# A new order for the first 740 steps of a hand-ordered retention and SwiGLU kernel

## The chip, the cores and the metric

One core of one Trainium2 chip runs the kernel. The metric is the device time of one execution in microseconds (us); lower is better. The engines have short names below: PE (TensorE, matrix products), DVE (VectorE), ACT (ScalarE), POOL (GpSimd) and SP (SyncE, which here does nothing but issue transfers).

## What is computed

Two blocks, one behind the other. The first is a recurrent retention over 4 batches, 8 heads, 768 positions and 64 values per head; the second is a SwiGLU feed-forward block over the 3,072 tokens that come out of it, with 512 model values and 1,536 inner ones.

```python
for t in range(S):                       # q, k, v: (4, 8, 768, 64)
    state = gamma[None, :, None, None] * state + np.einsum('bhd,bhe->bhde', k[:, :, t], v[:, :, t])
    y[:, :, t] = scale * np.einsum('bhd,bhde->bhe', q[:, :, t], state)
...
x = np.ascontiguousarray(attn_out.transpose(0, 2, 1, 3)).reshape(B * S, H * D)
...
g = x @ w_gate                           # (3072, 512) @ (512, 1536)
silu = g * (1.0 / (1.0 + np.exp(-g)))
val = x @ w_val
return (silu * val @ w_out).astype(np.float32)
```

The weights come as 8-byte numbers, because a float32 array is multiplied by a NumPy double when they are made; a load of one 128 x 512 piece is 512 KB.

## The kernel before

**Tiling.** The sequence is cut into 24 chunks of 128 positions (4 batches of 6). The chunks are worked through in four segments (`NSEG`) of six chunks each; a segment has 2 x 384 tokens. Each segment goes through three stages: retention of its six chunks, the up stage (gate and value products for 12 blocks of 128 inner values, SiLU, product) and the down stage (12 blocks, summed in six PSUM banks, one for each 128 tokens). Each float32 product is made from three passes of a narrower format: operands are split by `near_a`, `near_b`, `near_c` (weights and inner values) or `far_a`, `far_b`, `far_c` (inputs), the first on ACT, the second on DVE and the third on POOL or DVE.

**The first segment is special.** In it the weights are also loaded in 8-byte form, turned into float32, summed for a seven-product scheme that the later segments use, and kept in DRAM (`wup`, `wdn`, `wdnt`). So its up stage takes plain products (`plain`, `plain_part`). While its down stage runs, the retention of the second segment runs beside it.

**What sets the order.** Nothing is ordered by a scheduler at run time. `PLAN` is a string of 2,368 step names; `run` walks through it and issues what each name stands for. Each engine runs its own instructions in just the order in which they are issued, and waits by semaphores for what they need. A step thus has a place in the queue of each engine that it uses, and all that stands behind it on that engine waits with it. All loads and stores go out on SP's queue in order of the plan, apart from two loads of `q` that ACT issues at the very start. In the trace the transfers use eight semaphores in turn, and the issue of each waits until the transfer eight places before it has landed.

The steps that the text below names, with the line of the instruction in the trace:

- `l c:w` loads a chunk (0 to 5) of the first segment: `w` is 0 for keys, 1 for queries, 2 for values, 3 for keys by rows (256 KB each, line 485). `A n` loads a part of the decay table. `U f`, `V f` load weights (line 532): `f` 0 to 11 for the up blocks, 12 to 17 for pairs of down blocks. `Z` stores made weights (lines 503, 580), `P n` and `1/l n` load chunks of the second segment (line 935), `L` a column of decays.
- Retention: `s c` scores (PE line 651, DVE line 657), `o c` the old state's part (728), `m c` the new part and the first input split (742, ACT line 1138), `t c` the state's update (713; DVE line 718), `r c` transposes of keys (692), `x c:1`, `x c:2` the other two input splits (DVE). `q`, `k`, `K`, `Q`, `E`, `g` scale by decays.
- Weights: `a`, `b`, `c` (ACT lines 553, 556, 559), `S`, `C` (DVE lines 566 and 574, or POOL line 576) turn 8-byte words into float32; `n f:0` to `n f:5` split them; `T f:0` to `T f:2` sum them (DVE).
- Up stage: `p f:j`, `v f:j` are gate and value products for a third of the tokens (blocks 0 and 1, PE line 1075); `G f:i`, `W f:i` the same for half of the tokens (blocks 2 to 11, line 1057). `i f:i` is the SiLU (ACT), `j f:i` the product (DVE). `G f:i` uses bank `i`, `W f:i` bank `2 + i`; `G f:i` therefore waits until `i` of the block before has read its bank.
- Down stage of the first segment: `0/W f` loads down weights, `0/d f.0` to `0/d f.2` split them (ACT, POOL or DVE, DVE), `0/h f.0` to `.2` split the inner values, `0/D f.tok` multiplies (PE line 1301), `0/Z f` stores.
- Retention of the second segment: `1/sc`, `1/A`, `1/B`, `1/C` on PE (line 825), `1/dec`, `1/q`, `1/k`, `1/was`, `1/new`, `1/y`, `1/sum` and `1/x` on the other engines. `1/p f.n` are the seven products of its up stage (line 1230).

Of the kernel before, what the change touches and what calls it, by code (L numbers as in the profile page):

```python
# [25 lines left out]
L = 3  # L26
# [31 lines left out]
    C1:1 g3 b1:0 n1:0 v0:0 l5:0 U2:3 s5 S1:0 t3 c1:0 C1:0 l5:2  # L58
    p0:1 n1:1 u0:0 u0:1 T0:0 q5 v0:1 a2 l4:2 b2 y0:1 o5 y0:0
    o4 n1:3 S2 n1:2 m5 T0:1 n1:4 c2 m4 n1:5 x5:2 p1:0 l5:3  # L60
    x5:1 p1:1 u1:0 C2 v1:0 U3:1 T0:2 x4:2 T1:0 U12:0 a3 v1:1 y1:0
    x4:1 T1:1 L b3 p0:2 a12 c12 n2:0 S3 u1:1 T1:2 b12 u0:2
    U4:3 c3 Z0 n2:1 v0:2 Z1 n2:3 S12 y1:1 a4 n2:2 p1:2 v1:2
    C3 u1:2 n2:4 G2:0 y0:2 C12 G2:1 n3:0 U13:1 y1:2 n3:1 n2:5 b4
    T2:0 n3:2 S4 U5:2 n3:3 c13 T2:1 W2:0 Z12 W2:1 h0 c4 i2:1
    n3:4 i2:0 G3:0 n3:5 T3:0 C4 T2:2 T3:1 U6:3 j2:0 a5 G3:1 T3:2
    j2:1 Z2 n4:0 U7:0 W3:0 i3:0 n4:1 b5 n4:2 n4:3 S5 n4:4 W3:1
    i3:1 n4:5 c5 G4:0 C5 n5:0 a6 b6 a13 l4:3 T4:0 j3:0 G4:1
    n5:1 j3:1 Z3 T4:1 n5:3 i4:0 n5:2 T4:2 S6 W4:0 b13 c6 i4:1
    n5:4 a7 S13 C6 W4:1 n6:0 T5:0 U8:2 Z4 b7 U14:3 n5:5 n6:1  # L70
    G5:0 j4:1 S7 C13 j4:0 G5:1 n6:2 a8 n6:3 P2 n6:4 i5:1 c14
    W5:1 i5:0 Z13 c7 j5:1 T6:0 n6:5 W5:0 a14 U9:1 U15:0 C7 T5:1
    G6:0 T6:1 n7:0 T5:2 G6:1 n7:3 n7:1 T6:2 i6:0 b8 j5:0 Z5 S8
    n7:4 W6:1 b14 g4 n7:2 G7:0 i6:1 W6:0 P0 c8 S14 C8 Z6
    C14 h2 a9 b9 G7:1 j6:1 n7:5 S9 n8:0 c15 n8:3 j6:0 k5
    c9 W7:1 Z14 T7:0 n8:1 C9 n8:4 U10:2 a15 n8:2 i7:1 U11:1 W7:0
    T7:1 j7:1 n8:5 i7:0 T8:0 T7:2 b15 Z7 S15 a10 n9:0 G8:0 G8:1
    W8:1 i8:0 n9:3 b10 j7:0 T8:1 n9:1 n9:2 U16:3 S10 a11 n9:4 G9:0
    k4 i8:1 t4 C15 c10 C10 n9:5 W8:0 g5 n10:0 T8:2 T9:0 b11
    c16 n10:1 G9:1 Z15 j8:0 j8:1 n10:2 a16 n10:3 t5 U17:2 b16 W9:0  # L80
    i9:1 T9:1 0/h0.0 T9:2 S11 Z8 W9:1 S16 G10:1 n10:4 i9:0 C16 c11
    C11 n10:5 n11:0 j9:0 Z9 G10:0 n11:3 Z16 i10:1 j9:1 a17 i10:0 W10:1
    P1 n11:4 T11:0 T11:1 1/was0.0 T11:2 n11:1 W10:0 Z11 c17 n11:2 n11:5 b17
    0/h0.1 0/W0 G11:1 0/h1.0 G11:0 j10:0 0/d0.0 h1 0/h0.2 1/sc0 j10:1 i11:0 0/h1.1
    0/W1 S17 0/d1.0 i11:1 0/d0.1 1/l3 C17 T10:0 1/dec0.0 W11:0 0/d1.1 0/d0.2 W11:1
# [240 lines left out]
T0, UP0 = 30.0, 8.35  # L326
# [1176 lines left out]
```

## Time and profile before

| what | value |
|---|---|
| median of 3 runs | 639.5 us (638.78 to 642.62) |
| span of the profiled execution | 641.7 us |
| mean granted TensorE clock in it | 0.997 |
| first matmul of the first up stage (line 1075) | 22.87 us |
| first matmul of the first down stage (line 1301) | 132.25 us |
| first matmul of the second segment's up stage (line 1230) | 195.79 us |

The profile gives no time for the profiled execution besides its span; the span lies 2.2 us above the median of the runs and within their spread. Numbers with a place on the time axis are in us from the start of that span. A row of a timeline reads: start, duration, engine and line, operation, what it writes and reads, how many instructions the row joins, and in square brackets the idle time of the engine before it and what ended that. A row of a list of waits reads: who waited for whom, then total time, number of times and the longest.

### The profile page before, as it was taken

What the parts mean: (1) busy time and instruction counts of PE and PEld (TensorE: products, weight loads), DVE (VectorE), ACT (ScalarE), POOL (GpSimd) and SP (SyncE); (2) the same over time, 40 slices, a digit from 0 to 9 for tenths busy, and PEclk for the clock granted to TensorE, in tenths of its full rate; (3) what the DMA queues carried; (4) which work ended last, traced back from release to release, by engine and by line L of the source; (5) the groups of instructions that cost most, each with busy time, mean ns of one, the idle gap of its engine ahead of it and who ended that gap; (6) DMA issues with size and microseconds to landing.
All of it is one profiled execution on the core that took longest, in us unless ns stands there. A gap on an engine that the chain in (4) does not pass through costs nothing.

```text
span 641.7 us, 14131 instructions
## 1 busy us (share of the span) xinstructions
PE 630.8 (98%) x5601; PEld 581.7 (91%) x5601; DVE 506.9 (79%) x764; ACT 396.6 (62%) x845; POOL 173.2 (27%) x117
## 2 busy tenths in 40 slices
PE   7999999999999999999899999999999999999997
PEld 6899999987789999997788999998888999999886
DVE  4998788899898889887489777978778888877551
ACT  4786897677866665667376664756764655564220
POOL 0544455544423531210001343340002014232000
PEclk9999999999999999999899999999999999999999
DMA  9899998689788443688783435577785345304764
GB/s 319 289 353 311 372 333 274 259 323 305 281 278 305 140 157 115 214 263 239 204 312 130 179 115 206 173 203 229 229 290 196 113 149 189 128 13 140 230 212 149
DMA packets 57747, 143.03 MB, mean 223 GB/s; under 512 B 5840, under 2 KB 28368, under 8 KB 57680
## 3 DMA queue, kind: packets, MB, share of 16 engines
q1 hardware_dynamic: 57104, 141.33, 64.5%
q8 instruction: 44, 0.72, 0.5%
q10 hardware_dynamic: 576, 0.79, 0.3%
q14 instruction: 23, 0.19, 0.1%
HBM read 112.21 MB, written 29.88 MB: 221 GB/s over the span
## 4 chain that ended last, share of the span: by engine, by line
PE 94%; DMA 5%; ACT 1%; SPq 1%; issue 0%; DVE 0%; ACTq 0%
PE bank L1230 41%; PE bank L1301 30%; PE bank L1057 13%; PE bank L825 5%; PE bank L1075 3%; DMA oitem<-wdnt 2%; DMA hT<-in_v_n_dram 2%; PE bank L742 1%; DMA hT<-in_q_t_dram 1%; PE bank L728 0%; SPq L820 0%; PE bank L713 0%; PE bank L651 0%; ACT gitem L1129 0%; ACT local L871 0%
## 5 line engine op out<-in xcount | busy, mean ns | idle before, releaser
L1301 PE MATMUL bank<-oitem,gitem 128*128 128x512 f32 (+1 forms) x873 | 205.9, 393 | 3.0 <-DMA oitem<-wdnt 2.9
L1301 PEld LDWEIGHTS bank<-oitem,gitem 128*128 128x128 f32 x873 | 161.9, 189 | 38.1 <-DMA oitem<-wdnt 3.5
L1230 PE MATMUL bank<-xa,gitem 128*128 128x384 f32 x864 | 160.6, 334 | 0.0
L1230 PEld LDWEIGHTS bank<-xa,gitem 128*128 128x128 f32 x864 | 150.6, 188 | 0.1
L1135 POOL TENSOR_TENSOR gitem<-gitem 128x768 fp32r<-128x768 f32 x36 | 72.1, 2007 | 185.0 <-DVE gitem L1132 165.7
L1135 POOL TENSOR_TENSOR oitem<-oitem 128x512 fp32r<-128x512 f32 (+1 forms) x48 | 52.8, 1105 | 168.1 <-DVE oitem L1132 148.0
L418 DVE SCALAR_TENSOR_TENSOR gitem<-gitem 128x768 fp32r<-128x768 f32 x84 | 86.6, 1041 | 1.7 <-DVE gitem L1132 0.5
L1057 PE MATMUL bank<-xa,oitem 128*128 128x384 f32 x480 | 84.2, 335 | 0.0
L1230 PE MATMUL bank<-xb,gitem 128*128 128x384 f32 x432 | 83.7, 335 | 0.0
L1057 PEld LDWEIGHTS bank<-xa,oitem 128*128 128x128 f32 x480 | 83.0, 188 | 0.2
L1230 PEld LDWEIGHTS bank<-xb,gitem 128*128 128x128 f32 x432 | 75.8, 188 | 0.4
L1129 ACT ACTIVATE gitem<-loads 128x768 fp32r<-128x768 f32 x72 | 59.1, 842 | 25.7 <-PE bank L1230 16.9
L1132 DVE SCALAR_TENSOR_TENSOR gitem<-gitem,loads 128x768 fp32r<-128x768 f32 x72 | 70.5, 991 | 3.4 <-ACT gitem L1129 3.3
L1132 DVE SCALAR_TENSOR_TENSOR gitem<-gitem,hT 128x768 fp32r<-128x768 f32 x48 | 46.2, 965 | 28.0 <-ACT gitem L1129 24.1
L1129 ACT ACTIVATE gitem<-hT 128x768 fp32r<-128x768 f32 x48 | 40.2, 844 | 43.7 <-PE bank L1301 35.3
L1230 PE MATMUL bank<-xb,oitem 128*128 128x384 f32 x216 | 43.0, 335 | 0.0
L1230 PEld LDWEIGHTS bank<-xb,oitem 128*128 128x128 f32 x216 | 38.0, 188 | 0.0
L1246 ACT COPY tmp<-bank 128x384 f32<-128x384 f32 x36 | 17.3, 480 | 27.0 <-PE bank L1230 22.9
L1247 DVE TENSOR_TENSOR hT<-bank,tmp 128x384 f32<-128x384 f32 x36 | 20.0, 554 | 16.5 <-PE bank L1230 16.4
L1245 ACT COPY tmp<-bank 128x384 f32<-128x384 f32 x36 | 17.2, 479 | 24.8 <-PE bank L1230 17.1
L1249 DVE TENSOR_TENSOR hT<-hT,bank 128x384 f32<-128x384 f32 x36 | 19.7, 550 | 13.4 <-ACT bank L1249 13.2
L1247 ACT COPY tmp<-bank 128x384 f32<-128x384 f32 x36 | 17.3, 481 | 16.5 <-PE bank L1230 11.9
(152 smaller groups left out, 807.2 us busy)
## 6 DMA issues: line engine op xcount, KB each, us to landing
loads<-wup SPq DMA_DIRECT2D x36, 896.0 KB, 5.4
oitem<-wdnt SPq DMA_DIRECT2D x33, 768.0 KB, 4.7
wdnt<-oitem SPq DMA_DIRECT2D x12, 768.0 KB, 5.8
wup<-first SPq DMA_DIRECT2D x9, 896.0 KB, 6.9
rawp<-in_w_gate_dram SPq DMA_DIRECT2D x12, 512.0 KB, 7.3
rawp<-in_w_val_dram SPq DMA_DIRECT2D x12, 512.0 KB, 6.6
rawp<-in_w_out_dram SPq DMA_DIRECT2D x12, 512.0 KB, 5.8
out_dram<-chunk_x SPq DMA_DIRECT2D x21, 256.0 KB, 4.7
```

The costliest lines, as they stand in the source:

```text
L418: stt(o, x, 1.0, y, op0=mul, op1=op)
L825: nc.tensor.matmul(o, a, b, start=start, stop=True, skip_group_check=True)
L1057: nc.tensor.matmul(o, w[:, a, ts(b, P)], X0[:, a, i, NC - 1 - b], start=a == b == 0, stop=a == 2 and b == NC - 1, skip_group_check=True)
L1075: nc.tensor.matmul(o, w[:, a, ts(b, P)], X0[:, a, :, NC - 1 - b, ts(j, P)], start=a == b == 0, stop=a == 2 and b == NC - 1, skip_group_che ...
L1129: act(o[0], x, AF.Copy, scale=CUT / FAR)
L1132: stt(o[1], f32(o[0]), -FAR, x, op0=mul, op1=add)
L1135: op(o[2], f32(o[0]), f32(o[1]), op=add)
L1230: nc.tensor.matmul(o, w[:, a, k], x[:, a, KH - 1 - k], start=start and a == k == 0, stop=a == 2 and k == KH - 1, skip_group_check=True)
L1246: lambda: act(gate, c11, AF.Silu, scale=ONE), lambda: copy(u2, x),
L1247: lambda: copy(p5, wb), lambda: tt(h1, x, p5, op=add),
L1249: lambda: act(x, x, AF.Silu, scale=ONE), lambda: tt(h1, h1, x, op=mul))
L1301: nc.tensor.matmul(o, hs[g][:, a, ds(i * TH + u * P, P)], wo[g][:, a, cols], start=n == 0 and (f == 0 or final), stop=f == NF - 1 and a == ...
```

## The change

The first 740 names of `PLAN` are put in another order: 696 of the first 740 places hold another name than before, and from the 741st on the string is the same. The names are the same, each once. No function, size, buffer or number changes elsewhere. What a step does depends on the plan only where buffers are taken in turn: the two halves of banks 0 to 3 for `p` and `v`, the score buffers, and the slots of `item`, which go round in the order in which they are asked for.

The old string has 13 names a line and the new one is filled to a width, so that a diff shows every line as changed. Its beginning, old and new:

```diff
-    A0 I0 l0:0 l1:0 A2 A1 U0:0 s0 a0:1 r1 l0:2 s1 b0:1
-    A4 A3 l2:1 l2:0 r0 m0 K0 S0:1 c0:1 l1:2 x0:1 t0 s2
-    E1 l3:0 l3:1 m1 l2:3 C0:1 g2 V0:0 a0:0 Q2 n0:0 b0:0 l2:2
-    x1:2 s3 x1:1 n0:1 l4:1 l4:0 l3:2 t1 S0:0 k2 x0:2 q3 c0:0
-    C0:0 o2 U1:1 m2 o3 n0:3 s4 m3 a1:1 n0:4 x2:1 l5:1 l3:3
-    b1:1 x2:2 x3:1 S1:1 t2 n0:2 p0:0 q4 a1:0 x3:2 c1:1 n0:5 k3
...
+    A1 A2 l0:0 A0 l0:2 l1:0 s0 U0:0 a0:1 I0 l2:0 s1 A4 b0:1 r0 K0 m0 S0:1 l3:1 l2:1 A3 l1:2 x0:2 r1
+    E1 x0:1 s2 t0 c0:1 g2 m1 l3:0 t1 V0:0 Q2 l2:3 C0:1 s3 x1:1 l3:2 q3 l3:3 k2 l2:2 a0:0 b0:0 S0:0
+    x1:2 n0:0 l4:1 o2 c0:0 n0:1 o3 l4:0 m3 C0:0 U1:1 n0:3 t2 m2 x3:1 n0:4 k3 g3 x2:1 l5:1 x2:2 s4
+    a1:1 n0:2 b1:1 S1:1 c1:1 l5:2 x3:2 C1:1 a1:0 n0:5 b1:0 l5:0 U2:3 t3 n1:0 p0:0 S1:0 v0:0 l4:2 q4
```

The queue of each engine is what is left when the names of its own steps are picked out. For PE, up to the last retention group of the first segment:

```
old: s0 r1 s1 r0 m0 t0 s2 m1 s3 t1 o2 m2 o3 s4 m3 t2 p0:0 v0:0 s5 t3 p0:1 v0:1 o5 o4 m5 m4 p1:0
new: s0 s1 r0 m0 r1 s2 t0 m1 t1 s3 o2 o3 m3 t2 m2 s4 t3 p0:0 v0:0 p0:1 v0:1 s5 o5 o4 m4 m5 p1:0
```

For SP, up to the loads of the fourth chunk:

```
old: A0 l0:0 l1:0 A2 A1 U0:0 l0:2 A4 A3 l2:1 l2:0 l1:2 l3:0 l3:1 l2:3 V0:0 l2:2 l4:1 l4:0 l3:2 U1:1 l5:1 l3:3
new: A1 A2 l0:0 A0 l0:2 l1:0 U0:0 l2:0 A4 l3:1 l2:1 A3 l1:2 l3:0 V0:0 l2:3 l3:2 l3:3 l2:2 l4:1 l4:0 U1:1
```

Where the up stage goes over into the down stage, PE and DVE:

```
old PE:  ... W10:1 W10:0 G11:1 G11:0 1/sc0 W11:0 W11:1 0/D0.2 0/D0.1 0/D0.4 0/D0.0 1/A0
new PE:  ... W10:1 W10:0 1/sc0 G11:1 G11:0 W11:1 W11:0 0/D0.0 0/D0.1 1/A0
old DVE: ... n11:1 0/h0.1 j10:0 0/h0.2 j10:1 0/h1.1 S17 T10:0 1/dec0.0 0/d0.2 j11:0 j11:1 1/dec0.1
new DVE: ... n11:1 j10:1 0/h0.1 T10:1 0/h0.2 1/q0.0 j10:0 1/dec0.0 0/h1.1 S17 0/d0.2 j11:1 j11:0 1/dec0.1
```

Among the moves over a longer way: on ACT `c7` comes ahead of `i5:0`, and `g5` and `h1` are issued earlier; on POOL `k4` is issued earlier; on SP `l4:3` and `P0` are issued earlier and `L`, `P2` and `Z9` later; on PE the last retention group of the second segment, `1/C2`, comes ahead of six of the `0/D` groups that stood before it.

More of the change, by code (lines that the diff above doesn't have):

```diff
@@ L69 @@
[L69 to L85, printed above, removed]
@@ new lines @@
+    n3:2 T2:1 i2:0 n3:3 n3:4 i2:1 U5:2 T2:2 C4 n3:5 j2:0 j2:1 a5 C12 n4:0 b5 G3:0 G3:1 S5 T3:0 n4:3
+    P0 W3:1 W3:0 U6:3 Z2 Z12 n4:4 i3:1 c5 n4:1 i3:0 j3:1 n4:2 G4:1 C5 j3:0 U7:0 a6 T3:1 b6 T4:0 T3:2
+    n5:0 T4:1 S6 c13 a13 n5:1 i4:1 G4:0 n4:5 Z3 c6 n5:3 i4:0 n5:2 n5:4 h0 W4:1 W4:0 n5:5 T4:2 j4:1
+    C6 T5:0 b13 W5:1 S13 G5:1 j4:0 a7 G5:0 b7 h1 S7 i5:1 n6:0 n6:1 j5:1 C13 U8:2 c7 C7 n6:3 Z4 T5:1
+    W5:0 a8 n6:4 n6:2 U14:3 G6:1 c14 Z13 i5:0 T5:2 n7:0 G6:0 U9:1 b8 a14 j5:0 L S8 i6:1 n6:5 W6:1
@@ L198 @@
[L198 to L201 removed]
+    3/mv0.0 3/B0 3/dec2.1 3/dec2.0 2/W2 2/D2.1 3/l7 3/was0.11 3/was0.10 3/y0.10 3/y0.11 3/begin
```

313 lines of the change are left out of this document (159 added, 154 removed).

## The prediction

> **What bounds the kernel now.** I read the page's head and its chain by engine first, then TensorE's list of waits over the whole span, the windows of the stretch that the new order covers, and last the timelines of single engines there.
>
> ```profile
> span 641.7 us, 14131 instructions
> ...
> PE 630.8 (98%) x5601; PEld 581.7 (91%) x5601; DVE 506.9 (79%) x764; ACT 396.6 (62%) x845; POOL 173.2 (27%) x117
> ...
> PE 94%; DMA 5%; ACT 1%; SPq 1%; issue 0%; DVE 0%; ACTq 0%
> ```
> ```profile
> PE bank L1301 <- DMA oitem<-wdnt: 2.9, 1, 2.9
> PE bank L651 <- DMA hT<-in_k_t_dram: 1.7, 2, 1.1
> PE bank L742 <- DMA hT<-in_v_n_dram: 1.4, 2, 0.9
> PE bank L1420 <- DVE warm L1435: 1.1, 1, 1.1
> PE bank L651 <- DVE tmp L657: 0.4, 1, 0.4
> ```
> ```profile
> 0.00:10.00 10.00, 7.23 (x66) 6.31 (x68) 2.91 (x6) 2.15 (x3) 0.20 (x4) 1.00 0.82 282
> 10.00:20.00 10.00, 8.27 (x142) 7.11 (x144) 8.94 (x15) 7.37 (x22) 3.42 (x3) 1.00 1.07 373
> 20.00:30.00 10.00, 10.00 (x131) 9.31 (x127) 9.20 (x17) 7.68 (x17) 5.37 (x5) 1.00 0.85 292
> 40.00:50.00 10.00, 10.00 (x76) 10.00 (x75) 9.81 (x15) 8.21 (x14) 5.88 (x4) 1.00 0.92 340
> 70.00:80.00 10.00, 10.00 (x60) 10.00 (x59) 6.82 (x10) 7.12 (x10) 4.12 (x3) 1.00 1.00 357
> 140.00:150.00 10.00, 10.00 (x147) 7.95 (x146) 9.30 (x15) 8.03 (x26) 4.05 (x3) 1.00 0.90 317
> 170.00:180.00 10.00, 10.00 (x132) 8.05 (x124) 10.00 (x15) 6.70 (x16) 5.79 (x4) 1.00 0.82 280
> ```
>
> TensorE (PE) carries 94% of the chain. The columns of the windows are PE, weight loads, VectorE (DVE), ScalarE (ACT), GpSimd (POOL), clock, DMA share and GB/s. From 20 us on PE is busy in each of them, and the list of waits has only one PE wait behind the start, the 2.9 us on `wdnt`, in a part whose order stays. So the 740 steps cover a stretch in which PE has idle time in its first 20 us alone: 1.7 + 1.4 + 0.4 us there wait on transfers or on work that follows them (the 1.1 us before the warm-up comes ahead of the first step). The same window shows why: DMA at 1.07 of its engines' time, 373 GB/s. The start is paced by the order of the loads.
>
> **The change part by part.** No step is added or dropped, and no instruction changes its kind. The cost is in who waits for whom.
>
> *The start.* Here is PE's timeline, with the line of each group of matmuls:
>
> ```profile
> 5.93 1.16 PE L651 MATMUL bank<-hT 64*128 64x128 f32 x16 [1.14 <-DMA hT<-in_k_t_dram]
> 18.24 1.09 PE L742 MATMUL bank<-tmp,hT 128*64 128x128 f32 x16 [0.86 <-DMA hT<-in_v_n_dram]
> 19.27 1.09 PE L728 MATMUL bank<-loads,states 64*64 64x128 f32 x16
> 20.29 1.16 PE L651 MATMUL bank<-hT 64*128 64x128 f32 x16
> 21.38 1.09 PE L742 MATMUL bank<-tmp,hT 128*64 128x128 f32 x16
> 22.30 0.64 PE L713 MATMUL bank<-hT 128*64 128x64 f32 x16
> 34.49 11.78 PE L1075 MATMUL bank<-xa,oitem 128*128 128x256 f32 x96
> 46.11 58.41 PE L1057 MATMUL bank<-xa,oitem 128*128 128x384 f32 x336
> 132.25 3.13 PE L1301 MATMUL bank<-oitem,gitem 128*128 128x512 f32 x12
> ```
>
> The last wait of PE at the start ends at 18.24, when the values of chunk 2 (`l2:2`) land and `m2` can run. In the new order the same transfers stand ahead of `l2:2`, and two more, `l3:2` and `l3:3`, of 256 KB each. At the 373 GB/s of that window 524,288 bytes take 1.41 us, so `l2:2` lands at 18.24 + 1.41 = 19.65. For that, PE gets two groups done earlier that stood behind `m2`: `o3` (20.29 - 19.27 = 1.02 us) and `m3` (22.30 - 21.38 = 0.92 us), whose values now land ahead of `l2:2`. From 18.24 to `p1:0` at 34.49 PE has no wait, 16.25 us of work. So `p1:0` now starts at 19.65 + 16.25 - 1.02 - 0.92 = 33.96, 0.53 us earlier.
>
> A second, smaller term: a group of matmuls followed by one of the same array shape is shorter. `m3`, before `t2` of the same 128*64, takes 0.92 from start to start; `m2`, before `o3` of 64*64, takes 19.27 - 18.24 = 1.03. In the stretch left after `l2:2` the new order (`t2 m2 s4 t3 p0 ... s5 o5 o4 m4 m5 p1`) has seven changes of shape, where the old one without `o3` and `m3` has nine: two times 0.11 is 0.22 us. Together 0.75 us gained.
>
> Waits ahead of `l2:2` do not count in this sum, old or new (`s1` now has 512 KB more ahead of its keys, and will wait longer): they end before 19.65. Bounds of this part: it can gain no more than the transfer waits of the list without the one before `s0`, whose keys have the same 1,024 KB up to them as before: 1.7 + 1.4 + 0.4 - 1.14 = 2.4 us. And it loses 1.41 - 0.75 = 0.7 us if `l2:2` slips by as much again, two more 256 KB loads.
>
> *The stretch of the first matmul stage (46 to 132 us).* GpSimd and SyncE keep nearly their sequence. Weight loads `U7` and `U14` get 764 and 508 KB more ahead of them, at 357 GB/s 2.2 and 1.5 us. The nearest cover in the trace is this:
>
> ```profile
> 77.21 1.15 ACT L559 ACTIVATE rawp<-rawp 128x1024 int32<-128x1024 uint32 x1 [1.29 <-DMA rawp<-in_w_out_dram]
> 78.26 0.47 ACT L463 ACTIVATE tmp<-bank 128x384 f32<-128x384 f32 x1
> ```
>
> `c14` at 77.21 waits for `U14`, and `i5:0` (78.26 to 78.73) stands behind it and must free the bank of `G6:0`. `G6:0` is the 17th of 28 equal groups of the row at 46.11, so it starts at 46.11 + 16 x 58.41/28 = 79.49. With 1.5 us more, `i5:0` ends at 80.2; but `G6:0` comes behind `G6:1` now, one group (2.09 us) later, at 79.49 + 2.09 - 0.75 = 80.8. Hidden by 0.6 us; without that cover it would cost up to 1.5. Loads that move far (`l4:3` up, `P2`, `L` down) have cover on both sides: `P2`, the latest, now goes out right behind `P1`,
>
> ```profile
> 117.48 0.94 SPq L935 DMA_DIRECT2D loads<-in_q_t_dram x2
> ```
>
> which itself moves up; `P2` is first read by `1/A0`, behind 132 us. Counted at nothing.
>
> *Entry into the down stage.* This is the tightest place for VectorE:
>
> ```profile
> 118.28 0.69 DVE L1132 SCALAR_TENSOR_TENSOR oitem<-oitem,loads 128x512 fp32r<-128x512 f32 x1 [1.51 <-ACT oitem L1129]
> 122.90 0.56 DVE L463 TENSOR_TENSOR hT<-bank,tmp 128x384 f32<-128x384 f32 x1 [0.80 <-PE bank L1057]
> 128.98 2.31 DVE L1145 SCALAR_TENSOR_TENSOR oitem<-oitem 128x512 fp32r<-128x512 f32 x1
> 133.59 0.68 DVE L418 SCALAR_TENSOR_TENSOR loads<-loads,tab 128x512 f32<-128x512 f32 x1
> 138.33 1.50 DVE L418 SCALAR_TENSOR_TENSOR first<-first 128x256 f32<-128x256 f32 x1
> ```
>
> `0/d0.2` (128.98 to 131.29) makes the last part of the first down weights, 0.96 us before PE uses it at 132.25. Two steps are moved ahead of it: `1/q0.0` (0.68) and `T10:1` (1.50, the row at 138.33). If VectorE filled its queue without a gap, it would be late by 2.18 + 0.75 - 0.96 = 1.97 us. But VectorE stood idle for 1.51 + 0.80 = 2.31 us in this queue, and the two steps need neither of the things that it waited for. 2.31 covers 2.18, and what is left (0.96 - 0.75 = 0.21 us plus 0.13) is still positive. I take 0, with 2.0 us as the far end.
>
> *From there to 196 us.* The down groups and the second segment's retention come in another order, with the same work. VectorE is at 9.3 to 10.0 of 10 here, so it can just keep up with PE; the last retention group `1/C2`, behind which the next segment's inputs are summed, moves ahead of six down groups (row 132.25: 3.13/4 = 0.78 us each, so 4.7 us), which gives that end more room. 0, with up to 0.75 lost again where VectorE alone sets the end.
>
> Sum: 641.7 - 0.75 = 640.95 for an execution like the profiled one. That one is 2.2 us above the median of the runs, 639.5 (638.78 to 642.62); taken off the median it is **638.8 us**.
>
> **The rivals.**
>
> *VectorE late at the down stage (slower).* If the two idle stretches at 118 and 122 us don't fill, `0/d0.2` ends 2.0 us late and PE waits; with VectorE at 9.3 to 10.0 behind it, nothing makes that up: 639.5 - 0.75 + 2.0 = 640.8. It turns to a loss from 0.75 us of wait on. A longer wait has a further price here, which this trace has once:
>
> ```profile
> 305.00:310.00 5.00, 3.08 (x10) 2.47 (x11) 5.00 (x10) 2.80 (x8) 0.00 (x0) 0.82 1.05 261
> 310.00:315.00 5.00, 5.00 (x20) 4.07 (x19) 1.08 (x1) 0.00 (x0) 0.00 (x0) 0.84 0.30 89
> ```
>
> Behind the one wait of 2.9 us the granted clock was 0.82 and 0.84, a loss of 5 x 0.18 + 5 x 0.16 = 1.7 us. So a new wait of 3 us costs 4.7 and gives 639.5 - 0.75 + 4.7 = 643.5. The Trainium skill, page "TensorE: Matmul & The Clock Gate", section "Part 1: The HAM clock gate", says that PE falls to half clock after an idle window of about 3.4 us; by that rule a 3 us wait would mostly go free, and the time would stay at 641.8. The trace shows the drop behind 2.9 us. For this rival: the margins of 0.2 to 0.6 us above. Against: no wait of PE on VectorE but the 0.4 us of the list.
>
> *Nothing moves.* PE is full from 20 us, and VectorE at 10.00 in 170 to 180 could set the end whatever PE gains ahead: 639.5.
>
> *The start gains all (faster).* If both `s` and `m` waits fall away, 2.4 us: 637.1. If besides the 2.9 us on `wdnt` and its 1.7 us of clock fall out differently, 632.5. That part keeps its order, so I give it little.
>
> **How the numbers follow.** Forecast (637.8 to 640.2, its own 0.75 with the loss of 0.7 at the low end): 0.45. VectorE late or another new wait of the same kind (640.3 to 643.5): 0.28, and beyond, with several such waits and slow clock, above 645.9: 0.07. Nothing moves: 0.10, inside the forecast's range. Start gains all (636 to 637.8): 0.08; more than that, 0.02. The range 636.2 to 643.5 leaves out the two tails and the edge of the third case. One per cent is 6.4 us, about what a measurement of this kernel can tell from no change: faster than 633.1 needs the late wait and its clock as well, 0.02; slower than 645.9, 0.07; the rest, 0.91, within.
>
> **What would show it.** Right, if PE's wait for `in_v_n` ends near 19.7 us and is followed by an L713 group, L1075 x96 starts near 33.7 to 34.0 us, and L1301's first row has no wait, near 131.5. Wrong, if PE's list of waits gains a row on DVE, ACT or POOL between 25 and 196 us, or if the first L1230 row, at 195.8 before, is not earlier. A changed clock row near 308 us would move the time without saying anything on the order.

## The result, and the profile after

| | before | after |
|---|---|---|
| median, first set (15 runs each) | 639.31 us | 641.16 us |
| ratio, first set | | 1.0029 (95% interval 1.0016 to 1.0043) |
| ratio, a second set (12 runs against 26) | | 1.0041 (1.0022 to 1.0060) |
| profiled execution | span 641.7 us | 640.04 us, span 638.3 us |
| first `p1:0` product (line 1075; 1067 after) | 34.49 us | 34.91 us |
| first down product (1301; 1293) | 132.25 us | 132.85 us |
| first product of the second up stage (1230; 1222) | 195.79 us | 197.05 us |

The change costs about 2 us, 0.3%. That lies within 1% and in the range, but the forecast was a gain of 0.7 us, and a small loss came. The spans of the two profiles point the other way because the profile of before holds the 2.9 us wait on `wdnt` and its slow clock, which the profile of after doesn't have; up to the first product of the second up stage, where the orders meet again, the new one is 1.26 us behind.

In the new source each line number is 8 lower. TensorE's list of waits for the new kernel (who waited for whom: total us, times, longest) answers to that of before:

```profile
PE bank L643 <- DMA hT<-in_k_t_dram: 1.7, 2, 1.2
PE bank L1412 <- DVE warm L1427: 1.1, 1, 1.1
PE bank L1293 <- issue: 0.4, 1, 0.4
PE bank L817 <- issue: 0.2, 1, 0.2
```

The wait for the values, whose end the prediction moved to 19.65 us, isn't there at all. By this list alone the start has become better: 1.7 us of transfer waits in place of 1.7 + 1.4. PE's timeline shows what the list can't (start, duration, engine and line, operation, how many instructions, and the idle time before):

```profile
5.98 2.08 PE L643 MATMUL bank<-hT 64*128 64x128 f32 x16 [1.17 <-DMA hT<-in_k_t_dram]
8.62 2.08 PE L643 MATMUL bank<-hT 64*128 64x128 f32 x16 [0.55 <-DMA hT<-in_k_t_dram]
10.63 1.11 PE L684 MATMUL bank<-loads,hT 128*128 128x128 f32 x4
11.67 1.70 PE L734 MATMUL bank<-tmp,hT 128*64 128x128 f32 x16
13.30 0.66 PE L684 MATMUL bank<-loads,hT 128*128 128x128 f32 x4
13.89 1.16 PE L643 MATMUL bank<-hT 64*128 64x128 f32 x16
...
34.91 11.77 PE L1067 MATMUL bank<-xa,oitem 128*128 128x256 f32 x96
...
132.85 1.67 PE L1293 MATMUL bank<-oitem,gitem 128*128 128x512 f32 x6
141.24 3.79 PE L1293 MATMUL bank<-oitem,gitem 128*128 128x512 f32 x16 [0.39 <-issue]
197.05 2.27 PE L1222 MATMUL bank<-xb,gitem 128*128 128x384 f32 x12
```

Two things stand out. The groups of `s0` and `s1`, 16 equal matmuls each, take 2.08 us; the same group takes 1.16 at 13.89, and took 1.16 at 5.93 before. So PE ran at half clock until about 13 us, and from `s1` on was busy all that time, which is why no wait shows it. And `s1` starts at 8.62 (7.61 before), since its keys now come behind 512 KB more; from there to `p1:0` PE has no wait at all. The transfers no longer pace the start, PE does. The second thing is the stretch from the first down product to the second up stage: 197.05 - 132.85 = 64.20 us, where before had 195.79 - 132.25 = 63.54, with a wait of 0.39 at 141.24.

**The theory that follows.** (a) At the start: the late `s1` leaves PE idle between `s0` and `s1`, so the clock is half just where PE now has no slack, and that eats the gain. (b) In the down stage, the new order makes PE wait for split weights. The rival for (a): the order of loads and groups itself is worse, at any clock. The rival for (b): VectorE is full there, and any order in which PE comes earlier makes it wait. In the profile above the clock is half from `s0` on, ahead of the hole, so here the hole can only have kept it there; a fall behind the hole is seen in `start_new` and `new_again` below.

### The profile page after: what moved, and what is told of

It reads as the page before. It is cut to its first block, busy times and chain, and to the rows that moved or that the text cites. A ratio compares the mean times of both kernels' runs of the same rounds, so it can differ in the third digit from the quotient of the medians.

```text
span 638.3 us, 14136 instructions
## 1 busy us (share of the span) xinstructions
PE 631.5 (99%) x5601; PEld 583.2 (91%) x5601; DVE 506.9 (79%) x764; ACT 396.0 (62%) x845; POOL 174.6 (27%) x117
## 4 chain that ended last, share of the span: by engine, by line
PE 96%; DMA 2%; DVE 1%; SPq 0%; issue 0%; ACT 0%
PE bank L1222 41%; PE bank L1293 31%; PE bank L1049 12%; PE bank L817 6%; PE bank L1067 3%; PE bank L643 1%; PE bank L734 1%; DMA hT<-in_k_t_dram 1%; DMA oitem<-wdn 1%; PE bank L720 1%; PE bank L705 1%; PE bank L684 0%; DVE oitem L1137 0%; SPq L601 0%; DVE first L558 0%
## 5 line engine op out<-in xcount | busy, mean ns | idle before, releaser
L1124 DVE SCALAR_TENSOR_TENSOR gitem<-gitem,hT 128x768 fp32r<-128x768 f32 x48 | 49.4, 1034 | 22.2 <-ACT gitem L1121 18.3
L1238 ACT COPY tmp<-bank 128x384 f32<-128x384 f32 x36 | 17.3, 480 | 27.0 <-PE bank L1222 20.8
L1237 ACT COPY tmp<-bank 128x384 f32<-128x384 f32 x36 | 17.3, 480 | 24.1 <-PE bank L1222 16.4
L1133 POOL TENSOR_TENSOR oitem<-oitem 128x512 fp32r<-128x512 f32 x12 | 20.5, 1709 | 31.3 <-ACT oitem L1130 22.0
```

What stands on the lines that cost most here:

```text
L1124: stt(o[1], f32(o[0]), -FAR, x, op0=mul, op1=add)
L1133: op(o[1], f32(o[0]), x, op=sub)
```

## The experiments

Each kernel was timed in five rounds against the kernel before on the same chip, and profiled once. "Stretch" is the time from the first down product to the second up stage. The diffs show names of the plan, cut out of it without regard to its line breaks.

### Which part loses: each half alone

`start_new` takes the new order up to `p1:0` and then the remaining names as the old one has them; `start_old` the other way round.

```diff
-    A0 I0 l0:0 l1:0 A2 A1 U0:0 s0 a0:1 r1 l0:2 s1 b0:1
+    A1 A2 l0:0 A0 l0:2 l1:0 s0 U0:0 a0:1 I0 l2:0 s1 A4 b0:1 r0
...
+    y0:0 o5 o4 n1:3 n1:2 b2 S2 m4 m5 p1:0 T0:1 n1:4 c2 n1:5 x5:2 l5:3 x5:1 p1:1
```

> The new order up to p1:0, then the old order of all that is left. Theory A (the start is at fault: the hole between s0 and s1 leaves PE at half clock for s0, s1, r0 and m0): p1:0 starts about 0.4 us later than before (34.9 against 34.49 us), the first matmul of the second segment's up stage about 0.4 us later (196.2 against 195.79), time 0.4 to 1 us above the kernel before, and s0 and s1 take about 2.1 us each instead of 1.16. Theory B (the entry into the down stage is at fault): p1:0 no later than 34.5, time as before within 0.5 us. Theory C (nothing in the first 196 us, only the late wait on wdnt falls out more often): time as before or above it, with the first matmul of the second segment's up stage at 195.8.

> The old order up to p1:0, then the new order of all that is left. Theory A: p1:0 at 34.5, no waits of PE beyond those of before, time as before within 0.5 us. Theory B: p1:0 at 34.5, but 0/D0 and 0/D1 wait 0.4 us each as in the changed kernel, the second segment's up stage starts about 0.9 us later (196.7), time 0.9 us above the kernel before. Theory C: 195.8 and time as before.

Measured: `start_new` 641.12 us, ratio 1.0022 (1.0008 to 1.0037). `start_old` 640.43 us, 1.0010 (0.9996 to 1.0025). So the start with the old rest loses, clear of zero; for the rest alone a loss is likely in size but not clear. Not all of the first is the start: `start_new` comes to the second up stage at 197.88 us, 2.09 behind before, of which 0.86 is there at `p1:0` and 0.77 is a PE wait at 46.66, where its two orders are joined. `start_old` has `p1:0` at 34.12 and one wait of 0.41 us, at 160.18, not the two at the entry that theory B names (the new kernel's list has only one wait of 0.4 there). In `start_new` the windows view shows the clock (columns: stretch, length, then busy time of PE, weight loads, VectorE, ScalarE, GpSimd, the granted clock, DMA share, GB/s):

```profile
6.00:8.00 2.00, 1.11 (x16) 0.92 (x16) 0.85 (x2) 0.00 (x0) 0.00 (x0) 0.85 1.03 387
8.00:10.00 2.00, 1.45 (x14) 1.48 (x16) 0.57 (x2) 0.07 (x1) 0.00 (x0) 0.50 1.09 378
10.00:12.00 2.00, 2.00 (x14) 1.45 (x14) 1.37 (x3) 0.59 (x1) 0.00 (x0) 0.50 1.06 387
12.00:14.00 2.00, 2.00 (x19) 1.67 (x16) 1.21 (x2) 0.98 (x2) 1.17 (x1) 0.50 1.06 370
14.00:16.00 2.00, 2.00 (x35) 1.68 (x36) 1.66 (x3) 1.69 (x9) 0.10 (x1) 0.94 1.11 382
```

Here PE had full clock at `s0`, waited 1.44 us for `s1`, and ran at 0.50 from 7.4 to 14.2 us: 14 and 19 matmuls in 2 us in which PE is always busy, against 35 of another mix once the clock is back. The equal groups tell it more strictly: `s0` takes 1.16 us and `s1` 2.08. `p1:0` comes at 35.35 us.

### The clock alone: filling the hole

`new_warm` is the new kernel with five steps of warm-up matmuls (they multiply zeros, and nothing reads them) between `s0` and `s1`, and nine in place of seven ahead of the first step. `old_warm` has only the nine. `warm_start` is `start_new` with both.

```diff
-    A1 A2 l0:0 A0 l0:2 l1:0 s0 U0:0 a0:1 I0 l2:0 s1 A4 b0:1
+    A1 A2 l0:0 A0 l0:2 l1:0 s0 w w w w w U0:0 a0:1 I0 l2:0 s1 A4 b0:1
...
-    warm_up(7)
+    warm_up(9)
```

> The changed kernel with two more warm-up products ahead of s0 and five between s0 and s1, so that PE has no hole there (the products write a bank that nothing reads before it is written anew). Theory A: s0 and s1 take 1.16 us each, p1:0 starts at 33.7 to 34.0 us as forecast, and the time falls by about 1 us against the changed kernel, to 640.2. Theory B and C: s0 and s1 may be faster, but p1:0 or what comes behind it moves by less than 0.3 us and the time stays at 641.

> The kernel before with the two more warm-up products ahead of s0. A control for the one above: all theories expect no change, 639.3 within 0.5 us, with s0 at 5.9 to 6.0 us and 1.16 us long; if it is faster by 0.5 us or more, the old start too runs into the half clock in some executions.

> The new order up to p1:0 with the warm-up products that close the hole between s0 and s1, then the old order. Theory 1 (two faults: the half clock at the start, and the new order of the down stage, which keeps PE waiting): p1:0 at 33.4, first down matmul at 131.1, no PE wait in the down stage, 63.6 us in it, second segment's up stage at 194.7, time 1 us under the kernel before, 638.4. Theory 2 (VectorE or the transfers set the end of the down stage whatever the order): second segment's up stage stays at 195.8 to 196.5, time as before, 639.4, and PE waits in the down stage in the old order too.

Measured: `new_warm` 639.76 us, ratio 1.0007 (0.9992 to 1.0022); `old_warm` 639.22 us, 0.9993 (0.9981 to 1.0004); `warm_start` 639.30 us, 0.9994 (0.9974 to 1.0014). No load, buffer or data product differs between the new kernel and `new_warm`. PE's timeline of `new_warm`:

```profile
5.90 1.16 PE L644 MATMUL bank<-hT 64*128 64x128 f32 x16 [0.81 <-DMA hT<-in_k_t_dram]
6.99 1.38 PE L1413 MATMUL bank<-warm 128*128 128x128 f32 x10
8.37 1.16 PE L644 MATMUL bank<-hT 64*128 64x128 f32 x16
...
19.34 0.69 PE L706 MATMUL bank<-hT 128*64 128x64 f32 x16 [0.25 <-DMA hT<-in_v_n_dram]
...
33.35 11.77 PE L1068 MATMUL bank<-xa,oitem 128*128 128x256 f32 x96
```

`s1` is no earlier by more than 0.25 us (8.37 against 8.62), but it takes 1.16, and `p1:0` starts at 33.35, 1.56 us before that of the new kernel and 1.14 before the old one's. The rival for (a) falls, as far as `p1:0` is concerned. The old order with more warm-up has no gain to speak of (its `s0` took 1.47 us, its `p1:0` came at 34.62), so it isn't the longer warm-up as such.

### The same without extra work: the keys earlier

`new_k1` is the new kernel with one name moved; `start_k1` the same for `start_new`.

```diff
-    A1 A2 l0:0 A0 l0:2 l1:0 s0 U0:0 a0:1 I0 l2:0 s1
+    A1 A2 l0:0 l1:0 A0 l0:2 s0 U0:0 a0:1 I0 l2:0 s1
```

> The new order with one name moved: the load of the keys of chunk 1 (l1:0) goes out right behind that of chunk 0 (l0:0), as in the old order, ahead of A0 and l0:2. Theory (PE's clock falls because of the 1.4 us wait between s0 and s1): the keys of chunk 1 land about 1.4 us earlier, s1 runs at about 7.1 us without a long wait, s0 and the groups up to 14 us take their full-clock lengths (16 matmuls of scores in 0.9 to 1.2 us, none of 1.7), p1:0 starts at 33.3 to 34.0 us in place of 34.9, and the time is 1.0 to 1.5 us under that of the new order, 639.6 to 640.2, ratio 1.000 to 1.001. Rival (the start's loss is in the order of the values' loads or of PE's groups, not in the clock): s1 earlier, but p1:0 again at 34.8 to 35.3 us and the time at 641.1, ratio 1.003.

> The new order up to p1:0 with the keys of chunk 1 loaded right behind those of chunk 0, and the old order from there on. Theory (clock alone spoiled the start; the old order of the down stage adds no waits): like the start with filler products, but without them: full clock from 4 to 7 us on, p1:0 at 33.3 to 34.0 us, no PE wait between 130 and 196 us, first product of the second segment's up stage at 194.9 to 195.6 us, time 638.4 to 639.3, ratio 0.998 to 1.000. Rival (order of loads as such): p1:0 at 34.8 to 35.3, time 641.1, ratio 1.002.

Measured: `new_k1` 639.95 us, ratio 1.0003 (0.9982 to 1.0025), as the theory expected; `start_k1` 640.38 us, 1.0008 (0.9993 to 1.0022), over its range of 0.998 to 1.000. PE's timeline of `new_k1`:

```profile
6.05 2.06 PE L643 MATMUL bank<-hT 64*128 64x128 f32 x32 [1.23 <-DMA hT<-in_k_t_dram]
8.90 0.66 PE L684 MATMUL bank<-loads,hT 128*128 128x128 f32 x4 [0.80 <-DVE loads L677]
...
11.84 1.16 PE L643 MATMUL bank<-hT 64*128 64x128 f32 x16 [0.67 <-DMA hT<-in_q_t_dram]
...
33.32 11.77 PE L1067 MATMUL bank<-xa,oitem 128*128 128x256 f32 x96
131.08 1.55 PE L1293 MATMUL bank<-oitem,gitem 128*128 128x512 f32 x6
139.63 3.83 PE L1293 MATMUL bank<-oitem,gitem 128*128 128x512 f32 x16 [0.96 <-DVE first L410]
160.44 0.51 PE L1293 MATMUL bank<-oitem,gitem 128*128 128x512 f32 x1 [0.33 <-DVE oitem L1137]
...
196.41 2.27 PE L1222 MATMUL bank<-xb,gitem 128*128 128x384 f32 x12
```

The 32 matmuls of `s0` and `s1` run as one group, and `p1:0` starts at 33.32. `start_k1` gets 33.67, but then waits 1.06 us in two places at 42.9 and 45.3 us, where its two orders are joined, and is no clean test behind them. (`start_new` has 0.77 us at that joint, `warm_start` 0.17.)

### The hole in the old order

```diff
-    A0 I0 l0:0 l1:0 A2 A1 U0:0 s0 a0:1 r1 l0:2 s1 b0:1
+    A0 I0 l0:0 A2 A1 l0:2 l1:0 U0:0 s0 a0:1 s1 r1 b0:1
```

> The old order with the hole put in: the keys of chunk 1 are loaded behind A2, A1 and the values of chunk 0 (1,792 KB up to them, as in the new order), and s1 stands right behind s0, ahead of r1. Theory (clock): PE waits 1.3 to 1.5 us before s1, the clock falls to half from 7 to 8 us until 13 to 14 us, s1 and the next groups take 1.6 us or more in place of 0.9 to 1.2, p1:0 starts 0.5 to 1.7 us later than 34.5, and the time is 0.5 to 1.7 us over that of the old order, ratio 1.001 to 1.003. Rival (the transfers pace the start, and PE's clock ahead of the values of chunk 2 is hidden by their landing): s1 may be late and slow, but p1:0 stays at 34.3 to 34.6 and the ratio is 1.000.

Measured: 640.51 us, ratio 1.0009 (0.9992 to 1.0025), not clear of zero. In its profile `s0` and `s1` take 2.08 us each, the clock is full only from 10.2 us on, and `p1:0` starts at 35.00, 0.51 later than before. But the wait ahead of `s1` is 0.35 us, not the 1.3 to 1.5 that was expected, and the clock is half already at `s0`, ahead of it: this profile doesn't show a hole bringing the clock down, and the time leaves the theory open too.

### The unchanged new order again

> The new order unchanged, beside the three others on one chip. Theory (the wait ahead of s1 costs the clock): ratio 1.002 to 1.004 again; in the profile groups of scores of 1.6 us or more somewhere between 6 and 14 us, p1:0 at 34.7 to 35.4, and the stretch of the down stage at 64.2 us or more with PE waits of 0.3 us or more. Rival (the first profile caught the clock by chance): all groups at full-clock length, p1:0 at 33.3 to 34.0, and a ratio near 1.000.

Measured: 642.19 us against 640.20, ratio 1.0041 (1.0022 to 1.0060). PE's timeline:

```profile
6.03 1.16 PE L643 MATMUL bank<-hT 64*128 64x128 f32 x16 [1.21 <-DMA hT<-in_k_t_dram]
8.63 2.08 PE L643 MATMUL bank<-hT 64*128 64x128 f32 x16 [1.44 <-DMA hT<-in_k_t_dram]
...
34.24 11.77 PE L1067 MATMUL bank<-xa,oitem 128*128 128x256 f32 x96
131.99 1.55 PE L1293 MATMUL bank<-oitem,gitem 128*128 128x512 f32 x6
161.08 0.50 PE L1293 MATMUL bank<-oitem,gitem 128*128 128x512 f32 x1 [0.92 <-DVE oitem L1137]
...
197.02 2.27 PE L1222 MATMUL bank<-xb,gitem 128*128 128x384 f32 x12
```

This time `s0` had full clock, and the wait of 1.44 us came in front of a half clock from 8.3 to 11.7 us. `p1:0` starts at 34.24, earlier than the 34.7 to 35.4 that was expected. With the other profiles this gives the size of the effect. In `new_warm`, `p1:0` comes 33.35 - 8.37 = 24.98 us after `s1`, with 0.48 us of waits: 24.50 us of work at full clock. What a profile needs beyond that goes with the time that the clock stays half behind `s1`:

| kernel | `s1` at | clock full from | `p1:0` at | beyond `s1` + 24.50 | per us of half clock behind `s1` |
|---|---|---|---|---|---|
| new_again | 8.63 | 11.7 | 34.24 | 1.11 | 0.36 |
| after | 8.62 | 13.0 | 34.91 | 1.79 | 0.41 |
| new_sc0q (below) | 8.78 | 14.0 | 35.33 | 2.05 | 0.39 |
| down_old (below) | 8.49 | 14.3 | 35.33 | 2.34 | 0.41 |
| start_new | 8.55 | 14.2 | 35.35 | 2.30 | 0.41 |

Half clock by itself is not the loss. Two later kernels with early keys, `new_k1_l11` and `new_mended`, had half clock until 9.0 and 10.7 us and started `s1` at 7.8; their `p1:0` comes at 33.20 and 33.37. There the slow matmuls fill time in which PE would have waited for transfers anyway. It takes the late `s1` and the half clock together. Over all profiles `p1:0` comes at 34.12 to 34.62 us in five with the old start, at 34.24 to 35.35 in five with the hole in the new start, and at 33.15 to 33.67 in nine with that hole filled or closed.

The mean granted clock of every timed run shows how often it happens: one half window of 3.41 us in 640 lowers it by 0.0027, to 0.997. It was 0.997 or less in 27 of the 51 runs with the hole in the new start (after, new_again, start_new, down_old), in 3 of 12 of `old_hole`, and in 2 of 154 runs of before. With the new start and the hole closed or filled it was so in none of the 72 runs of six kernels (new_warm, warm_start, warm_down_old, new_k1, start_k1, new_k1_l11) and in 2 of 12 each of `new_mended` and `new_k1_sc0`. (The four later kernels of this list come below; `new_k1_sc0q`, `new_sc0q` and `down_new` are left out, since their waits of 1.8 to 2 us behind 130 us can lower their clock as well.) The count holds only falls that left a clock record: the profiled runs of after and `new_sc0q`, at half clock until 13.0 and 14.0 us, have means of 0.999 and 1.000.

### The down stage: splices

`down_old` is the new order through `W11:0` and then the old one, `down_new` the old one through `W11:1` and then the new; `warm_down_old` is `down_old` with the filled hole.

```diff
-    1/k0.0 0/d0.2 j11:1 1/k0.1 0/W1 W11:0 j11:0 0/D0.0 0/D0.1 0/d1.0 Z9 1/dec0.1
+    1/k0.0 0/d0.2 j11:1 1/k0.1 0/W1 W11:0 Z9 0/d1.0
...
```

> The changed kernel up to the last product of its first up stage, then the old order of all that is left; no extra warm-up. Theory 1: the down stage takes 63.5 to 63.8 us instead of 64.2, no PE wait there, time 0.7 us under the changed kernel. Theory 2: 64.2 or more as in the changed kernel, no gain.

> The old order up to the last product of the first up stage, then the new order of all that is left. Theory 1: PE waits of 0.3 to 0.5 us in the down stage, which takes 64.2 to 64.5 us instead of 63.5, time 0.7 us above the kernel before. Theory 2, or if the waits come from the order of the late up stage (loads and splits issued there): no PE wait, 63.5 us, time as before.

> The changed kernel with the warm-up products that close the hole, and the old order from the end of the first up stage on. Theory 1: p1:0 at 33.4, down stage from 131.1 in 63.6 us, time 1 us under the kernel before, 638.4, the fastest of all together with the warm new start alone. Theory 2: time as before.

Measured: ratios 1.0031 (1.0011 to 1.0050), 1.0060 (1.0038 to 1.0082) and 0.9998 (0.9981 to 1.0015). The splices add waits of their own right behind the joint: 0.76 and 0.78 us in `down_old`, 1.94 in `down_new`, 0.72 and 0.68 in `warm_down_old`. So they tell nothing on the down order; `warm_down_old` against `down_old` is the third pair in which the filled hole takes 0.3% away. The 638.4 us that theory 1 gave for `warm_start` and `warm_down_old` didn't come: 639.30 and 640.26.

### The down stage: single names

In the profiles without a joint there, the stretch is 63.53 to 63.97 us in six with the old down order and 64.20 to 65.78 in five with the new one (after 64.20, start_old 64.30, new_again 65.03, new_k1 65.33, new_warm 65.78), each of the latter with one to three waits of 0.3 to 1.0 us. Two places come again: near 140 us (after, new_k1), and near 160 (start_old, new_again, new_k1, new_warm); the longest stretch, that of `new_warm`, has two more, at 146.0 and 184.9. The rival for (b) doesn't hold: `warm_start` with the old down order and `new_k1_sc0` (below) with the new one come to the first down product at 131.47 and 130.90, before the 132.25 of the old kernel, and have no wait over 0.2 us in the stretch. The chain of waits of `new_again` goes back from the second one (start, duration, what):

```profile
146.30 6.37 DMA wdnt<-oitem
152.66 0.02 SPq L1267
152.69 0.03 issue
152.71 0.33 SPq L1267
...
154.08 3.52 DMA tmp<-in_k_n_dram
157.60 0.00 issue
157.61 0.04 ACT oitem L1130
...
160.43 0.07 DVE oitem L1137
```

The weight `0/W5` goes out at 152.71, when the store `0/Z2` of the weight that had its slot has landed, and the three transfers of `1/l11` go out right behind it (old: at 161.27, two weights later). At 157.61, 4.9 us later, ScalarE begins to split the weight (`0/d5.0`) after 2.31 us without work; VectorE's part follows, and PE's `0/D5.3` waits until 161.08. That the three transfers make the weight late is argued from this one chain: after and `new_k1_sc0` have `1/l11` in the same place and don't wait near 160.

Near 140 us the suspect was `0/W1`: its slot comes free with `G11:0`, and the new order has `1/sc0`, 1.1 us of PE, ahead of that. In the new kernel `0/W1` is issued 3.94 us ahead of the first down product.

Two kernels put `1/sc0` back behind `G11:0`. In `new_k1_sc0` it then reads queries that `1/q0.0` has already scaled, so the first scores of the second segment, and the output with them, are other values than they should be; `new_k1_sc0q` and `new_sc0q` (the latter with the late keys) move `1/q0.0` too. `old_sc0` puts `1/sc0` ahead of `G11:1` in the old order.

```diff
-    a17 n11:5 1/sc0 G11:1 b17 T10:1 0/h0.2 1/q0.0 i10:0 Z11 i11:1 G11:0 0/W0
+    a17 n11:5 G11:1 b17 T10:1 0/h0.2 1/q0.0 i10:0 Z11 i11:1 G11:0 1/sc0 0/W0
```
```diff
-    1/k0.0 0/d0.2 j11:1 1/k0.1 0/W1
+    1/k0.0 0/d0.2 j11:1 1/q0.0 1/k0.1 0/W1
```

> As new_k1, and 1/sc0 (the first scores of the second segment on PE) goes back behind both groups of the last up block, its place in the old order. Theory (1/sc0 ahead of G11 holds back the slot that the second down weight 0/W1 is loaded into, so that 0/d1 comes late and PE waits at 0/D1.0): no PE wait between 130 and 150 us, from the first down product to the second segment's up stage 63.5 to 63.9 us in place of 64.2 to 65.8, and the time 0.3 to 0.7 us under new_k1. Rival (the waits come from VectorE's order in the down stage as a whole, or from this piece only in part): waits of 0.3 to 0.6 us stay, the stretch is 64.2 us or more, and the time is that of new_k1 within 0.3 us.

> The new order with three names moved: l1:0 right behind l0:0; 1/sc0 behind both groups of the last up block; 1/q0.0, which scales the queries that 1/sc0 reads, behind j11:1, as in the old order. Theory (the new order loses in two places, the clock at the start and the slot of the second down weight behind 1/sc0): p1:0 at 33.2 to 33.8 us, first down product at 130.8 to 131.6, no PE wait over 0.3 us between 130 and 150 us, from there to the second segment's up stage 63.5 to 63.9 us, so that this begins at 194.4 to 195.4 us; time 638.0 to 639.2, ratio 0.997 to 0.999, under before and under the new order. Rival (what is gained ahead of 195 us is given back behind it, or the down stage sets its own pace): the stretch 64.2 us or more, or the same profile with a ratio of 1.000 or above.

> The new order with only 1/sc0 and 1/q0.0 moved back as above; the start with its wait ahead of s1 stays. Theory (two places): groups of scores of 1.6 us or more at the start, p1:0 at 34.7 to 35.4, first down product to second up stage 63.5 to 63.9 us in place of 64.2, ratio 1.001 to 1.0025, some 0.5 us under the new order. Rival (the start's clock is the whole loss in time): ratio as that of the new order in this set, within 0.0005.

> The old order with 1/sc0 moved ahead of both groups of the last up block, where the new order has it; nothing else. Theory (1/sc0 ahead holds back the load of 0/W1): that load goes out about 1.1 us later against the first down product than in the old order, PE waits 0.3 to 1.0 us in the first ten us of the down stage, that stretch takes 64.0 to 64.8 us in place of 63.5, ratio 1.0005 to 1.002. Rival (the wait comes from the rest of the new down order): no wait, 63.5 to 63.9 us, ratio 1.000.

Measured: `new_k1_sc0` ratio 0.9999 (0.9978 to 1.0021). `0/W1` goes out 5.23 us ahead of the first down product, the stretch is 63.77, and PE has no wait over 0.2 us in it: the profile looks as the theory asked, the gain in time over `new_k1` (0.0004) is not measurable. But the reason can't be `0/W1`. VectorE makes the last part of that weight (`0/d1.2`) at the same time in both kernels, first `new_k1`, then `new_k1_sc0`:

```profile
135.04 0.69 DVE L1137 SCALAR_TENSOR_TENSOR oitem<-oitem 128x512 fp32r<-128x512 f32 x1 [0.26 <-POOL oitem L1133]
135.04 0.69 DVE L1137 SCALAR_TENSOR_TENSOR oitem<-oitem 128x512 fp32r<-128x512 f32 x1 [0.43 <-POOL oitem L1133]
```

It is done at 135.73, 3.9 us before PE's wait in `new_k1` ends at 139.63, within the group `0/D1.0`. What PE waits for there stays open; the last section has a candidate. PE's busy time from 132 to 197 us (the sum line of the windows view) was 63.52 us in `new_k1` and here

```profile
sum 65.00, PE 64.68 PEld 51.96 DVE 60.78 ACT 45.60 POOL 25.38; mean PE 64.68 PEld 51.96 DVE 60.78 ACT 45.60 POOL 25.38
```

`old_sc0`: ratio 1.0014 (1.0000 to 1.0028), stretch 64.84, a wait of 0.46 at the first down product, sizes as expected. The way is another: PE waits there for VectorE's `j11:0`, which stands behind `0/d0.2`, and that ends 1.1 us later than before (132.37 against 131.29). `new_k1_sc0q`: 1.0037 (1.0016 to 1.0057); `new_sc0q`: 1.0080 (1.0057 to 1.0103). Both missed by far, through the new place of `1/q0.0`. VectorE's timeline of `new_k1_sc0q` has it at

```profile
131.50 2.46 DVE L410 SCALAR_TENSOR_TENSOR loads<-loads,tab 128x512 f32<-128x512 f32 x1
```

and GpSimd's, over the same time,

```profile
130.64 2.76 POOL L568 TENSOR_TENSOR first<-first,rawp 128x1024 int32<-128x1024 int32 x1 [2.14 <-ACT loads L960]
```

The step takes 2.46 us where it takes 0.68 elsewhere (124.96 in `new_k1`), `1/dec0.1` behind it (ahead of it in the old order) is late, and PE waits 1.98 us before `1/A0`, with half clock from 135.0 to 138.5. That is the tight entry of the prediction, met by a step moved in the other direction.

### Both places mended

`new_k1_l11` is `new_k1` with `1/l11` behind `1/l8`, as in the old order. `new_mended` also has `1/sc0` behind `G11:0`, `1/q0.0` behind `1/dec0.0` and `0/h1.1` behind `1/dec0.1`.

```diff
-    0/D3.5 1/l11 0/h5.2 0/d5.0
+    0/D3.5 0/h5.2 0/d5.0
...
-    1/y1.12 1/l8 1/y1.05 0/Z5 0/W7
+    1/y1.12 1/l8 1/l11 1/y1.05 0/Z5 0/W7
```

> As new_k1 (the new order with the keys of chunk 1 loaded right behind those of chunk 0), and the load 1/l11 goes back behind 1/l8, two down weights later, as in the old order. Theory (the three transfers of 1/l11 right behind the down weight 0/W5 make it land late, and PE waits near 160 us for 0/d5.2): no PE wait between 155 and 165 us; from the first down product to the second up stage 64.2 to 65.0 us in place of 65.3, as the wait near 140 us stays; second up stage at 195.3 to 196.1 us; ratio 0.998 to 1.000. Rival (the wait near 160 us hangs on the transfer behind which 0/W5 itself is issued, or PE only waits elsewhere): a wait of 0.3 us or more stays between 155 and 170 us, the stretch is 65 us or more, ratio 1.000 or above.

> As new_k1_l11, and at the entry of the down stage 1/sc0 goes behind both groups of the last up block, 1/q0.0 right behind 1/dec0.0 and 0/h1.1 behind 1/dec0.1. Theory (start's clock, the slot of 0/W1 behind 1/sc0, and 1/l11 are where the new order loses): p1:0 at 33.2 to 33.8, first down product 130.8 to 131.6 us, no PE wait of 0.5 us or more between 130 and 195 us, the stretch 63.5 to 64.2 us, second up stage at 194.4 to 195.6 us, ratio 0.996 to 0.9995, the fastest of all. Rival (VectorE is full there and any order that lets PE come a microsecond earlier makes PE wait for it, or what is gained ahead of 195 us is lost behind): waits of 0.5 us or more, the stretch 64.5 us or more, or the same gain in the profile with a ratio of 1.000 or above.

Measured: `new_k1_l11` has no wait near 160 us, a stretch of 63.92 and its second up stage at 194.87, all as the theory expected or better (a wait of 0.42 stays at 138.96). Its time doesn't follow: 641.19 us, ratio 1.0026 (1.0006 to 1.0047). `new_mended`, expected to be the fastest of all, has a new wait of 1.14 us at 146.93, a stretch of 64.67, and 639.98 us, ratio 0.9999 (0.9981 to 1.0017). No version beats the kernel before.

What lies behind 195 us moves by as much as all that was changed ahead of it. In the 20 profiles PE's waits there add up to between 0.0 and 3.1 us, nearly all at the same places in all orders: for `wdnt` between 294 and 316 us, near 446 to 458, and in two of them near 630. `new_k1_l11` had 1.97 us of them, `new_k1` had 0.53. A gain of 1 us at 195 us in one profile is therefore no proof of a gain in time.

## Why the prediction was wrong, step by step

- *What bounds the kernel.* Right: PE was full from 20 us on, and what went wrong lies in the first 14 us and where PE has no slack.
- *The start, the sum.* The terms held where the clock did, within 0.6 us. `l2:2` was to land at 19.65; the wait for it ends at 19.34 in `new_warm`, in front of the group that was named (L713, there L706). `p1:0` was to start at 33.74; it starts at 33.35, 33.32, 33.20 and 33.37 where the hole is filled or closed.
- *The step that failed:* "Waits ahead of `l2:2` do not count in this sum, old or new (`s1` now has 512 KB more ahead of its keys, and will wait longer): they end before 19.65." The longer wait was foreseen and priced at zero. But behind it PE has 24.50 us of work to `p1:0` and no wait that could take up a delay, so from 8.6 us on each us of half clock costs 0.4 us. PE comes to `t2`, the L713 group that was to start when `l2:2` lands at 19.65, only at 20.84 in after and 20.26 in `new_again`, without a wait: PE's own work had become the longer path. The forecast of -0.75 became -0.25 (new_again) and +0.42 us (after) against the 34.49 of before; the start of before itself varies between 34.12 and 34.62 in five profiles.
- *The clock rule, used in the wrong place.* The prediction had a drop of the clock behind 2.9 us of wait, and used it only as the price of a new 3 us wait in the down stage. The Trainium skill, page "TensorE: Matmul & The Clock Gate", section "Part 1: The HAM clock gate", calls half clock the default, says that it rises after a busy window of about 3.4 us and falls after an idle one, and that the windows run free of the kernel's start. The free-running windows agree with the traces: the same kernel got full clock at 13.0 us in one profile and at 4.9, and again at 11.7, in another. The idle window doesn't: the clock fell with no idle time longer than 1.44 us, behind windows in which PE was busy for about half of the time or less (last section).
- *The up stage, counted at nothing.* Right. From `p1:0` to the first down product before took 97.76 us, after 97.94, the repeat 97.75, and the lists of waits have no PE wait there. `U7`, `U14`, `l4:3` and `P2` cost nothing.
- *The entry into the down stage, 0 taken.* Right in that the first down product has no wait in the new kernel, but not by the margin of 0.2 us that was worked out: `0/d0.2` ends at 133.27, 0.42 us after that product has begun at 132.85. Only the third of its three passes reads the part that `0/d0.2` makes, and that pass comes later still. So this end came out right by luck. How tight VectorE is there shows in `new_k1_sc0q`, at `1/A0`.
- *From there to 196 us, "0, with up to 0.75 lost again where VectorE alone sets the end".* The loss was 0.66 us in one profile, within what was allowed, and 1.49 in the other, twice that. The reason given was not the one seen: in the other profile VectorE stood idle for 2.24 us until 158.55, while ScalarE waited for transfers, `0/W5` and `1/l11`. The sum was argued from the list of waits of before, where no such wait is; the margins of the weights' landings were not looked at, though `0/W` is a step that the change moves against SP's queue.
- *The rivals.* "VectorE late at the down stage" was nearest in sign and size (640.8 to 643.5); its place and mechanism were not what happened. Of the rest, "start gains all" is excluded by the medians.

Shown: the hole ahead of `s1` and the half clock together, as the part of the loss that timing can see. In three pairs that differ in the warm-up products alone the ratio falls from 1.0022 to 0.9994, from 1.0029 to 1.0007 and from 1.0031 to 0.9998 (the last pair timed against the same runs of before; in the first the joint at 46 us adds to the difference). Against it stands `new_k1_l11`, whose hole is closed and which is still slower, 1.0026. Shown in profiles only: the longer stretch of the down stage. Argued: `0/W5` behind `1/l11` as the reason near 160 us. Open: the reason near 140 us; and why the 1.1 us that the closed hole brings at `p1:0` are not seen as time in any kernel; the down stage takes some of it back, and the waits behind 195 us differ by more than that between single runs.

## What to carry to other kernels

A wait that "ends before the wait that counts" isn't free if PE has no slack behind it: ask what the engine still has to do after it, and at which clock. An order worked out from transfers, banks and copies with one speed for TensorE can trade a short hole at the start for a better transfer order; count the hole at both speeds, and fill it or load first what ends it. A wait that goes away with an edit isn't yet explained by it: look whether what it was said to wait for came earlier. And read the durations of equal groups beside the list of waits: half clock is busy time, and no wait shows it.

## What the runs showed of the hardware

**The clock comes in windows.** The trace records the granted clock in stretches. Between the first change and the last in each profile they are whole multiples of 3,413 ns: half clock for one or two of them (8.3 to 11.7 us in `new_again`, 7.4 to 14.2 in `start_new`, 308.2 to 311.6 before, 135.0 to 138.5 in `new_k1_sc0q`), full clock for 1 to 186. Carry the bounds on as a grid, and PE's busy time in a window (windows view) goes with the clock in the next one. In the 20 profiles the clock fell behind every full-clock window in which PE was busy for 1.64 us or less, behind none with 1.83 or more, and did either between 1.69 and 1.80. At half clock it rose behind every window with 2.90 us or more, and behind none with 2.86 or less. So it fell in `new_again` behind 4.9 to 8.3 us, which has both waits in it (1.16 us busy), and in the profile of after, at half clock already, the rise was missed behind 6.1 to 9.5 us, where the wait of 0.55 us leaves 2.86. Single waits of 2.87, 1.98 and 1.77 us brought a fall and left 1.28, 1.60 and 1.64 us of work in their window; waits of 1.97, 1.94, 1.65 and 1.64 us brought none and left 1.69 to 1.78. This is read from runs made for other ends, and no run varied the share on purpose. At the start the clock came up between 4.0 and 14.0 us, the late ones in kernels with a hole, apart from 9.0 and 10.7.

**PE waits that no engine ends.** The profiles label 15 of PE's waits behind 20 us "issue", `0/D1.0` near 140 us in after and `new_k1_l11` and places near 445 to 451 us among them. By the times in the traces, each of the 15 ends 2.4 to 2.9 us after a 16 KB transfer of kind "instruction" (queue q8 of the DMA view, 44 in the whole run of after) has started; the wait near 140 us in `new_k1`, labelled with a VectorE step, ends 2.2 us after one. That PE waits for its own instructions there fits, and was not tested.

**A view that hides it.** The trace of after holds no clock record before 13.0 us, and the windows view shows 1.00 there, as does the span's mean of 0.999. Only the 2.08 us in place of 1.16 tell.

**VectorE behind GpSimd.** The 0.68 us step that took 2.46 us started at 131.50 while a GpSimd step ran from 130.64 to 133.40, and ended at 133.96, 0.56 us after it. In `new_k1`, where the step takes 0.68 us at 124.96, GpSimd runs nothing from 123.9 to 126.9 us. The Trainium skill, page "SBUF — State Buffer", section "SBUF: two separate sides", says that a VectorE instruction with two inputs in SBUF and a GpSimd one that reads SBUF lock each other out for a whole instruction; that is what these two rows look like.
